# Scans two blocks ahead, a new order of ScalarE's copies, and three early expert jobs in one attention and mixture-of-experts kernel

## The chip, the cores and the metric

The kernel runs on one core of a Trainium2 chip. The metric is device time in microseconds (us), the median of the timed runs. Engines are named as the profile names them: PE is TensorE (PEld its weight loads), DVE VectorE, ACT ScalarE, POOL GpSimd, and SP the engine that issues most transfers.

## The reference

For 4 batches, 8 heads, 768 tokens and head dimension 48, a gated linear attention with a decay for each element, and then a mixture of 8 experts over the 384 columns of its output:

```python
for t in range(S):
    state = alpha[:, :, t, :, None] * state + np.einsum('bhd,bhe->bhde', k[:, :, t], v[:, :, t])
    y[:, :, t] = np.einsum('bhd,bhde->bhe', q[:, :, t], state)
...
fresh_e = int(np.argmax(logits[b, s]))
if s == 0 or local_gate[b, s] < 0.5:
    e = fresh_e
else:
    e = prev_e if prev_e >= 0 else fresh_e
...
h = np.maximum(x[b, s] @ w1[e], 0.0)
out[b, s] = p[e] * (h @ w2[e])
```

Each of the 3072 tokens goes to one expert (384 to 1024 to 384 columns), picked by its own logits or carried over from the token before, and is scaled with its softmax weight.

## The kernel before, in words

**Attention.** The tokens are cut into 24 blocks of 128 (two chunks of 64); block i belongs to batch i % 4, so a batch's state comes back every fourth block. The main loop makes 26 iterations, `for i in range(NB + 2)`, and keeps every instruction in the order in which it is written. One iteration touches several blocks:

- `scan1(i+1)`: POOL writes ones into four columns of the decay tile `a`; DVE scans the decays into `A` and takes reciprocals; POOL multiplies q by `A`.
- `kt(i)`, `pm(i)`: PE transposes k (kp), ACT copies it (kk); PE makes the products of k and q inside a chunk (pe), DVE masks them (pq).
- `scan2(i+1)`: DVE scans backwards into `sf`, POOL multiplies k by it.
- `xt(i-2)`: PE transposes the finished rows (xp), ACT copies them (xx); every fourth time a router `route(g)` starts.
- `ym(i-1)`: PE forms y from the states `sb` and from `pq`, ACT copies it to `XR`; SP stores it to `xd` in device memory.
- `um(i)`: PE forms the state update (up), DVE adds it to the state `st`, ACT copies the state to `sb` (two copies), and DVE starts the batch's next state.
- `first_v(i+1)`: ACT copies half of a v tile.

`load_a`, `load_x`, `load_v` are issued on SP for coming blocks; SP takes its queue in order.

**The router and the early jobs.** Three times in an iteration `other()` first emits what was put off in `later` (the low parts of splits, the stores of results), then one piece of each open router, then one piece of the early expert work; until there is such work, two matmuls on zeros (`dz`) stand in its place. A router works in 14 pieces over four blocks; its last ones scatter four blocks of list entries to `ls` (four indirect DMAs on POOL). When blocks 0 to 11 are listed, `early()` begins: it runs expert 0 and then expert 1 on the first C1 = 240 rows of their lists. A `Job` loads its list (SP), gathers token rows from `xd` (POOL), transposes them (tp) and splits them into xh and xl, and then runs `gemm1` (8 pieces of 9 matmuls) and `gemm2` (2 slices of 24 matmuls for 240 rows).

**Weights.** Each expert's weights come in 7 pieces (3 of w1, 128 x 1024, and 4 of w2, 128 x 768). Four raw buffers (`rw`) are shared; ACT casts a piece to the high part, and the low part is a subtraction, on POOL for w1 and on DVE for w2. Expert 0's pieces begin in block W0 = 4, one in each block, three asked for ahead; expert 1's begin in the second half of the first early job. There are four buffers for w1 parts and six for w2 parts.

**Expert phase.** After the loop come the remaining jobs with their own pools, in the order of the list in line 645: the rest of expert 1 (240 rows), experts 2 to 7 (480 rows each), the rest of expert 0. Here the order is not pinned.

Almost all operations pass through one wrapper, so the profile gives them line 78 (79 after the change); they are known by tile names.

## Time and profile before

| | us |
|---|---|
| timed runs | 541.92, 546.92, 548.57 (median 546.92) |
| the profiled execution's own time | 534.36 |
| its span, first to last instruction | 532.6 |
| first matmul of block 0 (kp), of block 20 | 13.34, 179.15 |
| last matmul | 519.28 |

Busy time over the span: PE 450.3 (85%), DVE 261.5 (49%), ACT 180.0 (34%), POOL 225.4 (42%); the mean granted clock of PE is 0.901.

How to read it: a busy share is an average over stages with different limits, so the span is cut into stages, and in each the engine that the others wait for is looked for. "Idle before, releaser" is the time that an engine stood before an instruction, and what ended it. The granted clock is the share of full speed that PE was given; at a low clock the same matmuls take longer and count as busy longer. Matmuls overlap, so the length of one is not its cost.

### The profile page before, as it was taken

The page shows a single profiled execution, that of the slowest core. Times are in us where ns is not written, and L with a number is a line of the kernel's source. Part 1 is how long each engine was busy: PE and PEld are TensorE (multiplying, and loading weights), DVE is VectorE, ACT ScalarE, POOL GpSimd, SP SyncE. Part 2 cuts the span into 40 slices and gives each one's busy share as a digit, 9 for nine tenths or more (in the row PEclk, how much of TensorE's full clock was granted, in tenths as well). Part 3 has the DMA queues.
Part 4 walks back from the last instruction along what each step waited for, and adds up shares of the span by engine and source line. Part 5 has one row for each costly group of instructions (what it writes and reads, how often), then busy time and mean ns, then how long its engine had stood idle before and what let it go on. Part 6 is the DMA issues. An engine that isn't in the chain of part 4 may idle for free. (4 is left out here: it accounts for less than half of the span.)

```text
span 532.6 us, 10859 instructions
## 1 busy us (share of the span) xinstructions
PE 450.3 (85%) x4391; PEld 404.1 (76%) x4391; DVE 261.5 (49%) x445; ACT 180.0 (34%) x350; POOL 225.4 (42%) x240
## 2 busy tenths in 40 slices
PE   4986879798686787963959989999999999999990
PEld 4764758576575676753949979999899998999990
DVE  3675696686887645263313443533425334243320
ACT  1243353434343333443103443342323433343110
POOL 6335344435254641093242637344372543633301
PEclk9898796789796688995878999999999999999996
DMA  9656465535455441376121545525345263360100
GB/s 204 131 162 233 138 200 137 142 108 142 130 164 124 135 87 43 122 185 173 50 53 53 163 138 148 179 74 167 117 122 174 84 189 115 103 191 14 46 3 25
DMA packets 30059, 66.15 MB, mean 124 GB/s; under 512 B 7694, under 2 KB 13979, under 8 KB 30007
## 3 DMA queue, kind: packets, MB, share of 16 engines
q1 hardware_dynamic: 23478, 54.42, 36.7%
q0 software_dynamic: 4864, 10.66, 6.9%
q8 instruction: 35, 0.57, 0.5%
q10 hardware_dynamic: 1665, 0.35, 0.4%
q14 instruction: 17, 0.14, 0.1%
HBM read 55.89 MB, written 10.70 MB: 125 GB/s over the span
## 5 line engine op out<-in xcount | busy, mean ns | idle before, releaser
L78 DVE SCALAR_TENSOR_TENSOR hl<-h,hh 128x480 fp32r<-128x480 f32 (+1 forms) x80 | 44.2, 554 | 80.4 <-ACT hh L78 80.4
L78 ACT ACTIVATE hh<-h 128x480 fp32r<-128x480 f32 (+1 forms) x80 | 39.0, 489 | 87.2 <-PE h L78 86.9
L78 POOL DMA_INDIRECT xg<-xd,li x32 | 35.2, 1099 | 50.4 <-DMA li<-ls 33.3
L78 POOL TENSOR_TENSOR x<-x,A 112x512 f32<-112x512 f32 x24 | 28.3, 1179 | 65.4 <-PE pe L78 16.7
L78 POOL DMA_INDIRECT out<-yo,li x32 | 33.5, 1048 | 50.1 <-DVE yo L78 44.2
L78 POOL TENSOR_TENSOR x<-x,sf 112x512 f32<-112x512 f32 x24 | 30.8, 1282 | 29.7 <-DVE sf L78 25.0
L78 DVE TENSOR_SCALAR yo<-yp,li 120x384 f32<-120x384 f32 x32 | 19.5, 616 | 47.0 <-PE yp L78 47.0
L78 ACT COPY sb<-st 48x384 f32<-48x384 f32 x48 | 24.5, 511 | 48.7 <-DVE st L78 48.1
L78 DVE TENSOR_TENSOR_SCAN A<-a,z 112x520 f32<-112x520 f32 x24 | 29.7, 1239 | 20.4 <-POOL a L78 18.9
L78 DVE TENSOR_TENSOR_SCAN sf<-a,z 112x520 f32<-112x520 f32 x24 | 37.8, 1574 | 0.0
L78 PE MATMUL h<-dz 128*128 128x240 f32 x138 | 34.7, 362 | 2.3 <-DVE z L78 2.3
L78 POOL DMA_INDIRECT ls<-pl,ix x24 | 24.0, 1000 | 26.0 <-DVE ix L78 19.3
L78 PE MATMUL xp<-cs,XR 128*128 128x128 f32 x72 | 15.8, 339 | 19.9 <-ACT kk L78 19.9
L78 PE MATMUL y<-vt,pq 64*64 64x48 f32 x768 | 32.4, 243 | 0.0
L78 DVE TENSOR_TENSOR st<-up,st 112x384 f32<-112x384 f32 (+1 forms) x24 | 12.5, 522 | 40.2 <-PE up L78 33.1
L78 PEld LDWEIGHTS y<-vt,pq 64*64 64x64 f32 x768 | 29.3, 158 | 3.6 <-issue 1.5
L78 PEld LDWEIGHTS h<-dz 128*128 128x128 f32 x138 | 24.3, 235 | 6.1 <-DVE z L78 2.3
L78 PEld LDWEIGHTS xp<-cs,XR 128*128 128x128 f32 x72 | 9.7, 166 | 22.9 <-ACT kk L78 22.7
L78 PE MATMUL y<-sb,x 112*64 112x96 f32 x384 | 26.1, 290 | 0.2 <-ACT sb L78 0.2
L78 PE MATMUL tp<-cs,xg 120*128 120x120 f32 x96 | 15.2, 290 | 13.0 <-DMA xg<-xd,li 7.1
L78 ACT COPY XR<-y 128x384 f32<-128x384 f32 x24 | 11.5, 479 | 42.1 <-PE y L78 42.1
L78 PEld LDWEIGHTS y<-sb,x 112*64 112x64 f32 x384 | 20.9, 164 | 5.7 <-issue 5.2
(229 smaller groups left out, 1260.0 us busy)
## 6 DMA issues: line engine op xcount, KB each, us to landing
x<-akq SPq DMA_DIRECT2D x24, 448.0 KB, 5.1
a<-akq SPq DMA_DIRECT2D x24, 227.9 KB, 4.5
vt<-vn SPq DMA_DIRECT2D x24, 192.0 KB, 2.4
xd<-XR SPq DMA_DIRECT2D x24, 192.0 KB, 4.2
rw_0a<-w SPq DMA_DIRECT2D x3, 512.0 KB, 5.8
rw_0a<-w SPq DMA_DIRECT2D x4, 384.0 KB, 4.9
rw_1a<-w SPq DMA_DIRECT2D x3, 512.0 KB, 4.2
rw_1a<-w SPq DMA_DIRECT2D x4, 384.0 KB, 5.9
```

The costliest lines, as they stand in the source:

```text
L78: r = f(*a, **k)
```

## The change

What it does:

1. **Scans.** The memset of `a` becomes a function of its own, `one_a`. In iteration i, `scan2(i+1)` comes first, then `one_a(i+2)`, and `scan1(i+2)` stands after the first `other()`: the decay scan runs two blocks ahead. `a` and `A` get three buffers, x five; `load_a` and `load_x` both fetch block i+3.
2. **Copies.** `um` ends with the add. The two copies of the state (`copies`) and the next state's start (`state`) are done for block i-1 in the next iteration, behind `kt(i)`. `first_v` moves ahead of `um`.
3. **y.** `ym` does the 16 products with `pq` first, and then the 8 with `sb`; the store to `xd` is issued by ACT right behind the copy to `XR`.
4. **Weights.** Expert 0's first four pieces are loaded in block 2, and used one per block from block 5. `Weights` has an argument for the engine of w1's low part: DVE for experts 0, 1 and 2, whose weights are begun inside the loop or by the early jobs. Expert 1's first four pieces are loaded when the early lists are.
5. **Early jobs.** There are three, in written order: expert 0, expert 1 (240 rows each), and the rest of expert 1, whose list is loaded when all routers are done. The transposes of the next job stand inside `gemm2` of the one before, through a PSUM tag of another block ("tr"). Expert 2's weights follow the first job, and the expert phase begins with expert 2. `other()` also gives only one piece at a time while a router is still open after the loop.

The diff, cut to its core:

```diff
-W0 = 4
+W0 = 2
 NP = 3
-NX = 4
+NX = 5
...
+    a_ = s_
...
-                self.defer(lambda e=g_ if n < 3 else v_, lo=lo, rw=rw, hi=hi:
+                self.defer(lambda e=self.sub if n < 3 else v_, lo=lo, rw=rw, hi=hi:
...
-            g_.memset(a[:, C + 1:SW:2 * (C + 1)], 1.0)
-            A = ap.tile([R, SW], F32, tag="A", bufs=2, name=f"A_{i}")
+            A = ap.tile([R, SW], F32, tag="A", bufs=3, name=f"A_{i}")
...
+        def one_a(i):
+            a = blk[i]["a"]
+            g_.memset(a[:, C + 1:SW:2 * (C + 1)], 1.0)
...
+        def copies(i):
+            sf, sb = blk[i]["s3"].rearrange("p c h d -> p c (h d)"), blk[i]["sb"]
             s_.copy(sb[64:112, :, 0, :], sf[64:112, 0:2])
             s_.copy(sb[0:48, :, 1, :], sf[0:48, 0:2])
...
             s_.copy(d["XR"], yw[:, 0:DM])
+            a_.dma_start(xd[1 + i * 128:1 + (i + 1) * 128], d["XR"])
...
+        def begin(e):
+            EW[e] = Weights(e, f"{e}a", 4, later.append, v_)
+            for _ in range(4):
+                EW[e].load()
...
+            jobs = [Job(e, r, n, m1, pp, 2, 2, 8, 2, (0, 1, 1), rows, 1, later.append)
+                    for e, r, n, rows in ((EARLY[0], 0, C1, 1 + T1 * 128), (EARLY[1], 0, C1, 1 + T1 * 128),
+                                          (EARLY[1], C1, CAP - C1, NTOK + 1))]
...
+                    if k % 4 < 2 or k == 2:
+                        next(ws, None)
+                    if nx and k > 3:
+                        if nx.r0 and k == 4:
+                            while steps:
+                                yield False
+                            nx.load_list()
+                        if nx.r0 and k == 5:
+                            nx.gather()
+                        if k == (7 if nx.r0 else 5):
+                            for _ in nx.trans():
+                                yield True
...
+                if n == 0:
+                    begin(NEXT)
...
         for i in range(NB + 2):
             if i + 1 < NB:
-                scan1(i + 1)
+                scan2(i + 1)
+            if i + 2 < NB:
+                one_a(i + 2)
             if i < NB:
                 kt(i)
+            if 0 < i <= NB:
+                copies(i - 1)
+                state(i - 1)
+            if i < NB:
                 pm(i)
-            if i + 1 < NB:
-                scan2(i + 1)
-            if i + 2 < NB:
-                load_a(i + 2)
             if i > NB:
                 drained[0] = True
             other()
+            if i + 2 < NB:
+                scan1(i + 2)
+            if i + 3 < NB:
+                load_a(i + 3)
+                load_x(i + 3)
...
+            if i == W0:
+                begin(EARLY[0])
+                wsteps = EW[EARLY[0]].steps()
+            elif i > W0 + 2:
+                next(wsteps, None)
             other()
             if i < NB:
                 um(i)
-            if 0 < i <= NB:
-                y_.dma_start(xd[1 + (i - 1) * 128:1 + i * 128], blk[i - 1]["XR"])
```

Where it moves instructions, in the names that follow the number behind a tile's name is the block, the router's group or the weight piece; x is the tile of k and q.

POOL, where the second router's four scatters (`ls`) fall, before:

```order
L78 TENSOR_TENSOR x_14_1416<-x_14_1416,A_14_1552 112x512
L78 TENSOR_TENSOR x_14_1416<-x_14_1416,sf_14_1582 112x512
L78 DMA ls_77<-pl_1_1480,ix_1_1587 24960x3 x4
L78 MEMSET a_15_1585 112x4
L78 TENSOR_TENSOR x_15_1522<-x_15_1522,A_15_1682 112x512
```

and now:

```order
L79 TENSOR_TENSOR x_14_1386<-x_14_1386,A_14_1490 112x512
L79 TENSOR_TENSOR x_14_1386<-x_14_1386,sf_14_1554 112x512
L79 MEMSET a_15_1494 112x4
L79 DMA ls_77<-pl_1_1481,ix_1_1588 24960x3 x4
L79 TENSOR_TENSOR x_15_1496<-x_15_1496,A_15_1596 112x512
L79 TENSOR_TENSOR x_15_1496<-x_15_1496,sf_15_1684 112x512
```

The memset of block 15's decays stood behind the scatters and now stands ahead of them; behind them now stands the q product of block 15, while PE is at block 13.

DVE, one turn of the loop near the same place, before (pq of block 12):

```order
L78 TENSOR_TENSOR st_11_963<-up_11_1421,st_11_963 112x384
L78 SCALAR_TENSOR_TENSOR st_15_1433<-st_11_963,A_11_1227 112x192
L78 SCALAR_TENSOR_TENSOR A_13_1443<-a_13_1375,z1_84 112x520
L78 RECIPROCAL z2_85<-A_13_1443 112x4
L78 TENSOR_TENSOR pq_12_1471<-pe_12_1454,cs_66 128x512
L78 SCALAR_TENSOR_TENSOR sf_13_1473<-a_13_1375,z2_85 112x520
```

and now (pq of block 13):

```order
L79 TENSOR_TENSOR st_12_1105<-up_12_1539,st_12_1105 112x384
L79 SCALAR_TENSOR_TENSOR sf_14_1554<-a_14_1384,z2_85 112x520
L79 SCALAR_TENSOR_TENSOR st_16_1567<-st_12_1105,A_12_1274 112x192
L79 TENSOR_TENSOR pq_13_1586<-pe_13_1569,cs_66 128x512
L79 TENSOR_TENSOR ps_1_1589<-pw_1_1549,ps_0_1127 128x40
L79 TENSOR_TENSOR po_1_1591<-ps_1_1589,oh1_105 128x32
L79 TENSOR_REDUCE ix_1_1588<-po_1_1591 128x4
L79 SCALAR_TENSOR_TENSOR A_15_1596<-a_15_1494,z1_84 112x520
L79 RECIPROCAL z2_85<-A_15_1596 112x4
```

The scan A is now of the block two ahead of pq and stands after the router's steps; the scan sf stands right behind the add, with the next state's start (st_16) between it and pq.

ACT, where the first weight piece is cast (w1h_0a_0), before:

```order
L78 COPY sb0_97<-st_4_247 48x2x192 x2
L78 COPY vt2_95<-vt2_95 64x384
L78 CAST w1h_0a_0_632<-rw1_0a_0_626 128x1024
L78 COPY kk_5_645<-kp_5_640 128x448
L78 COPY xx_0_380<-xp_3_674 128x384
L78 COPY XR_4_704<-y_4_679 128x384
```

and now:

```order
L79 COPY kk_5_646<-kp_5_641 128x448
L79 COPY sb0_97<-st_4_268 48x2x192 x2
L79 COPY xx_0_389<-xp_3_681 128x384
L79 COPY XR_4_711<-y_4_686 128x384
L79 DMA xd_76<-XR_4_711 128x384
L79 COPY vt0_91<-vt0_91 64x384
L79 CAST w1h_0a_0_716<-rw1_0a_0_425 128x1024
L79 COPY lc_0_733<-lg_0_720 128x128
```

The cast stood ahead of kk of block 5 and now stands behind block 5's kk, behind the store that ACT issues itself; the copies of sb follow kk.

## The prediction

> **What bounds the kernel now.** I read the table of stages first, cut at the matmuls that open blocks 0, 5, 13 and 20 (kp), at the end of the last block's work, and at the steady expert phase. Each row gives the stage and its length in us, then busy us (and instructions) of PE, PE's weight loads, DVE, ACT and POOL, then PE's granted clock, DMA share and GB/s.

> ```profile
> 13.34:44.28 30.94, 26.91 (x491) 21.96 (x492) 21.90 (x29) 11.33 (x24) 12.82 (x19) 0.93 0.55 142
> 44.28:119.16 74.88, 59.44 (x939) 49.42 (x938) 54.98 (x89) 29.94 (x65) 33.42 (x35) 0.79 0.55 162
> 119.16:179.15 59.99, 44.77 (x811) 36.96 (x809) 44.18 (x76) 22.58 (x55) 29.84 (x35) 0.85 0.54 140
> 179.15:229.40 50.25, 43.30 (x612) 37.23 (x612) 24.69 (x58) 19.98 (x44) 14.94 (x18) 0.87 0.36 101
> 229.40:293.00 63.60, 44.39 (x278) 41.41 (x279) 22.88 (x54) 15.46 (x36) 26.18 (x23) 0.79 0.38 96
> 320.00:520.00 200.00, 199.62 (x1108) 188.00 (x1105) 75.70 (x120) 66.77 (x108) 84.06 (x59) 1.00 0.39 115
> ```

> From 320 us on PE is full and at full clock; nothing there changes but names. The losses lie before 293: PE is idle and its clock is low. In the same view, block by block, the blocks without routing or weights (the first two rows) take 6.35 and 6.56 us; the third row is the block in which the first weights begin, the fourth one with a routing scatter.

> ```profile
> 31.37:37.72 6.35, 5.50 (x112) 4.53 (x110) 4.76 (x6) 2.82 (x6) 2.53 (x4) 1.00 0.59 170
> 37.72:44.28 6.56, 5.50 (x111) 4.52 (x110) 4.76 (x7) 2.82 (x6) 2.48 (x5) 1.00 0.59 172
> 44.28:57.61 13.33, 8.45 (x137) 6.94 (x135) 4.60 (x7) 4.13 (x8) 4.79 (x4) 0.74 0.68 219
> 126.12:137.56 11.44, 6.06 (x114) 5.01 (x113) 7.11 (x15) 3.19 (x8) 6.15 (x8) 0.85 0.62 164
> ```

> So a smooth block is 0.85 us above its PE work, and a disturbed one loses 5 to 7 us. The timeline of the scatter's block says why (start, length, engine, operation, and in brackets the idle time before it and its releaser):

> ```profile
> 125.81 1.05 POOL L78 DMA_INDIRECT ls<-pl,ix  x1 [1.08 <-DVE ix L78]
> 129.71 0.97 POOL L78 DMA_INDIRECT ls<-pl,ix  x1 [0.30 <-issue]
> 130.67 0.13 POOL L78 MEMSET a<- 112x4 f32 x1
> 130.84 1.24 DVE L78 TENSOR_TENSOR_SCAN A<-a,z 112x520 f32<-112x520 f32 x1 [4.06 <-POOL a L78]
> 134.57 1.17 POOL L78 TENSOR_TENSOR x<-x,sf 112x512 f32<-112x512 f32 x1 [1.18 <-DVE mx L78]
> 134.60 1.18 DVE L78 TENSOR_TENSOR ge<-L,mx 128x32 f32<-128x32 f32 x1
> 135.82 0.19 DVE L78 TENSOR_TENSOR ge<-ge,cs 128x32 f32<-128x32 f32 x1
> 136.74 0.60 PE L78 MATMUL rp<-cs,kr 128*32 128x128 f32 x2 [4.59 <-DVE kr L78]
> ```

> Four scatters hold POOL from 125.81 to 130.67; a four-column memset stands behind them, the scan behind the memset, the router behind the scan, and PE loses 4.59 us. The two `ge` rows show a second thing: the same operation takes 0.19 us alone, but 1.18 us when POOL's multiply (134.57 to 135.74) is running.

> **The change part by part.** *Scans two ahead.* The memset now precedes the scatters, and the scan and decay product of block i+2 are made in iteration i. What then waits for a scatter is POOL's q product, a block before PE needs it: 130.67 - 125.81 = 4.9 us of scatter against some 6.5 us of slack. I cost the scatter at nothing; if the cover is gone it costs the old 4 us, four times. What is late next is DVE's own turn, below.

> The floor of a block is PE's work at full clock plus the smooth 0.85. Blocks 13 to 19: 44.77 x 0.85 = 38.1, over 7 blocks 5.4, so 6.3 each. I add 0.7 for routing, whose DVE steps (134.60 to 136.69, half of it lock) still stand between pq and the next scan: 7.0 x 7 = 49, against 59.99. **Gain 11.** Bounds: 16 with nothing added, 2 if DVE sets the pace.

> DVE's turn of a block comes from these groups (mean ns of one) and POOL's two products:

> ```profile
> L78 DVE TENSOR_TENSOR_SCAN sf<-a,z 112x520 f32<-112x520 f32 x24 | 37.8, 1574 | 0.0
> L78 DVE TENSOR_TENSOR_SCAN A<-a,z 112x520 f32<-112x520 f32 x24 | 29.7, 1239 | 20.4 <-POOL a L78 18.9
> L78 POOL TENSOR_TENSOR x<-x,A 112x512 f32<-112x512 f32 x24 | 28.3, 1179 | 65.4 <-PE pe L78 16.7 <-issue 14.5 <-PE kp L78 12.6
> L78 DVE TENSOR_TENSOR pq<-pe,cs 128x512 f32<-128x512 f32 x24 | 16.1, 672 | 7.6 <-PE pe L78 7.5
> ```

> `sf` alone is as long as `A`; its mean of 1574 is a wait for the q product. In the new order: sf 1.24, state 0.36 to 0.47, pq 0.67, A 1.24, then the product 1.18, with the add of st inside it: 4.8 us if state gets in ahead of POOL's k product, 6.0 if it waits that out. With about 0.9 of routing that is 5.7 to 6.9, near PE's 6.3: DVE is the engine to watch. I take the lower, because state stands directly behind sf on DVE, while POOL first has to be signalled.

> [...]

> *First weights from block 2.* Before, the first weight is asked for and used in one block:

> ```profile
> 44.18 1.86 SPq L78 DMA_DIRECT2D rw_0a<-w  x3
> 49.23 1.04 ACT L78 CAST w1h_0a<-rw_0a 128x1024 fp32r<-128x1024 f32 x1 [3.06 <-DMA rw_0a<-w]
> 28.74 1.14 PE L78 MATMUL y<-vt,pq 64*64 64x48 f32 x32
> 50.76 0.90 PE L78 MATMUL xp<-cs,XR 128*128 128x128 f32 x3 [4.88 <-ACT kk L78]
> 53.07 1.95 PE L78 MATMUL y<-vt,pq 64*64 64x48 f32 x32
> 62.22 3.46 DVE L78 TENSOR_TENSOR ge<-L,mx 128x32 f32<-128x32 f32 x1
> 63.30 2.34 POOL L78 TENSOR_TENSOR w1l_0a<-rw_0a,w1h_0a 128x1024 fp32r<-128x1024 f32 x1
> ```

> ACT waits 3.06 us for the transfer with kk behind it, PE loses 4.88 us and goes on at a low clock (1.95 us for a y group that took 1.14 at 28.74). Asked for three blocks earlier, that wait goes. The three subtractions of 2.34 us leave POOL (one holds DVE's `ge` for 3.46 us) and become DVE's: a 768-wide one takes 0.93 us there (row below), so 1.24 each for 1024, and all seven steps now stand behind scan A and thus behind the q product.

> ```profile
> L78 DVE TENSOR_TENSOR w2l_0a<-rw_0a,w2h_0a x4: 925/928/932, 79.4 to 108.4; 128x768 fp32r<-128x768 f32 x4
> ```

> Blocks 5 to 12: 59.44 x 0.79 = 47.0, 5.9 a block, 6.7 with 0.85; plus about 1.2 for the subtraction and its lock: 7.9 x 8 = 63, against 74.88. **Gain 12**; bounds 21 with nothing added, 0 if lock and clock stay. The four loads (1.9 MB) now go ahead of block 6's inputs in SP's queue; block 5 lost 7 us to such a collision and ACT's wait together, so up to 4 of it may return. It is inside the bounds.

> *ACT's order, y's order, stores on ACT.* kk now precedes the two copies of sb, and y begins with the 16 products that don't need sb; both hide under PE's 0.85 and cost nothing. The store leaves SP for ACT:

> ```profile
> L78 SPq DMA_DIRECT2D xd<-XR x24: 319/379/3215, 23.4 to 226.7; - x24
> DMA to landing us min/median/max: 1.9/4.2/6.1
> ```

> Issue 0.38 us on ACT, which is busy 2.82 of 6.35: hidden, with 3 us to spare. In exchange the second expert's loads no longer stand in SP's queue behind stores. Start: one more scan (1.24 us) ahead of the first add: **1 us lost**.

> *Blocks 20 to 23 and the last xt, ym.* 43.30 x 0.87 = 37.7, plus 2 us for 12 more matmuls of the first job, plus 6 x 0.85: 45 against 50.25. **Gain 5**, bounds 0 and 8.

> *The tail.* Where the first early job ends, PE waits three times:

> ```profile
> 241.54 0.86 PE L78 MATMUL tp<-cs,xg 120*128 120x120 f32 x3 [5.91 <-DVE xl L78]
> 249.21 0.83 ACT L78 CAST w2h_2b<-rw_2b 128x768 fp32r<-128x768 f32 x1 [6.04 <-DMA rw_2b<-w]
> 251.40 0.57 PE L78 MATMUL h<-xh,w1h_1a 128*128 128x240 f32 x1 [5.44 <-DVE hl L78]
> 260.97 1.02 POOL L78 DMA_INDIRECT ls<-pl,ix  x1 [15.85 <-DVE ix L78]
> 276.51 1.43 PE L78 MATMUL tp<-cs,xg 120*128 120x120 f32 x6 [5.03 <-DMA xg<-xd,li]
> ```

> and the granted clock of the second wait and behind the third, by stages:

> ```profile
> 246.00:251.40 5.40, 0.00 (x1) 0.00 (x1) 1.33 (x3) 1.91 (x4) 0.00 (x0) 0.50 0.51 203
> 276.50:284.20 7.70, 6.66 (x29) 6.04 (x30) 1.95 (x4) 1.75 (x4) 5.33 (x5) 0.50 0.45 128
> ```

> The first two are ACT standing at weights that have not landed, and PE then runs at 0.50. Expert 1's weights are now begun some five blocks earlier, and expert 2's casts stand in the third job, not ahead of the second job's Relu: 5.91 + 5.44 and about 4 of slow clock go, of which I leave 2 standing. The third wait is a chain of four scatters, list, gather (260.97 to 276.51, 15.5 us) behind the last routing; the third job needs the same list, so its 5 us stay. New: at the first job of the expert phase ACT has two w2 casts that need the third job's last matmul, then four xh casts and a w1 cast: about 5 us, where the present kernel loses little. 5.91 + 5.44 + 4 - 2 = 13.4, less these 5, plus the 2 us of matmuls done earlier: **gain 10**; bounds 0 and 17. The third job itself is the same PE work as the first job of the expert phase was, so it moves no time of its own.

> Sum: 11 + 12 - 1 + 5 + 10 = **37 us** off the profiled execution, whose own time is 534.36 (span 532.6). The three timed runs have a median of 546.92, 2.4% above it; taking the same microseconds off gives **510**.

> **The rivals.** *A slow clock stays and DVE paces* (B): PE's busy time stays 59.44 and 44.77, and state and the subtractions wait out every product, 1.1 us more in 15 blocks. 59.44 + 8 x 0.85 and 44.77 + 7 x 0.85 save 18, of which 16 are lost again: 2 - 1 + 5 + 10 = 16 in all, **531**. For it: DVE has 54.98 of 74.88 now. Against: its waits are mostly those removed.

> *Full clock everywhere* (C): the bounds 16 and 21 hold, 16 + 21 - 1 + 5 + 10 = 51 in all, **496**. It needs PE gaps short enough to keep 1.00, as the two smooth rows with 0.85 us of gaps have. [...]

> *The waits only move* (E): B's blocks, and the tail's 10 come back at the list and at expert 2's weights: 16 - 10 = 6 off, **541**. It is also the case in which the lookahead is one in name only, because the a tiles land too late:

> ```profile
> a<-akq SPq DMA_DIRECT2D x24, 227.9 KB, 4.5
> ```

> Against that, a third buffer lets SP ask for a tile over a block (6 us) before its memset, and landing takes 4.5.

> *Slower* (D): ACT is in order, and at each store stands until an earlier transfer has landed. At 6.1 us, the longest landing, a block of ACT is 2.82 + 0.38 + 6.1 = 9.3 us, 1.8 over the forecast's mean of (49 + 63) / 15 = 7.5, and 24 blocks take 43 us more: **553**. ACT sets the pace from a hold of 4.3 us, the present time is passed at 5.8, and 2% over it at 6.3. Against it: the awaited transfers are some two blocks old.

> **How the numbers follow.** Forecast 0.58, B 0.16, C 0.12, E 0.07, D 0.07. About 2% can be told from no change, here 11 us: below 536 is faster. Faster: 0.58, 0.12 of B, 0.12: 0.82. Same: 0.04 of B, 0.07, 0.03 of D: 0.14. Slower: the rest of D, 0.04. The range, 491 to 533, takes in C and most of B and leaves E and D out.

> **What would show it.** Right: no idle of DVE behind POOL's memset; scatter blocks within 1.5 us of smooth ones; no ACT wait on rw_0a or rw_2a with PE idle; kp of block 20 some 22 us earlier; a 5 us wait of PE for the third job's gather still there. Wrong: block time set by DVE's subtractions behind POOL, a clock under 0.85 before block 20, or ACT idle at its stores.

## The result and the profile after

The changed kernel takes 511.94 us, median of four runs (508.97 to 513.86), against 544.42 for four runs of the kernel before (538.47 to 548.57): ratio 0.947, 95% interval 0.937 to 0.958, faster. The profiled executions lie closer together: 513.54 after (span 511.7) and 534.36 before. The times below are of single executions unless a ratio stands with them. Executions of one program differ by up to 3%, the longer ones at a lower granted clock (those of the kernel before that ran beside e12 go from 532.94 us at 0.904 to 548.62 at 0.874); ratios leave the slow ones out, and the profiled executions of e1 and e11 are slow ones.

The table of stages of the changed kernel, cut at the same events as before (kp of blocks 0, 5, 13 and 20, the last router matmuls lg, then a piece of the tail and the steady phase):

```profile
12.72:42.05 29.33, 27.06 (x491) 22.60 (x492) 21.06 (x29) 12.12 (x25) 12.97 (x19) 0.89 0.84 234
42.05:98.02 55.97, 51.52 (x939) 43.05 (x938) 48.23 (x89) 30.61 (x65) 26.21 (x32) 0.91 0.68 185
98.02:148.04 50.02, 44.79 (x811) 36.95 (x809) 37.12 (x77) 21.56 (x49) 28.00 (x33) 0.90 0.60 167
148.04:207.98 59.94, 43.99 (x623) 36.74 (x623) 27.34 (x63) 22.65 (x50) 17.64 (x21) 0.91 0.37 95
207.98:271.60 63.62, 49.78 (x291) 46.47 (x291) 22.55 (x54) 15.39 (x34) 22.35 (x23) 0.81 0.31 86
299.00:500.00 201.00, 199.68 (x1105) 188.05 (x1103) 74.57 (x117) 65.43 (x105) 84.81 (x60) 1.00 0.38 114
```

Blocks 0 to 4 went from 30.94 to 29.33 us, blocks 5 to 12 from 74.88 to 55.97, blocks 13 to 19 from 59.99 to 50.02. Kp of block 20 stands 31.1 us earlier (148.04 for 179.15). Then the stage from block 20 to the last lg, 229.39 - 179.15 = 50.2 us before, takes 59.9: 9.7 of it are lost again. From there to the end it is 303.7 us for 303.2: the tail gained nothing.

In the attention blocks the forecast waits are gone. The scatter's block, from the timeline (start, length, engine, operation, idle before it and releaser):

```profile
103.30 1.23 DVE L79 TENSOR_TENSOR_SCAN A<-a,z 112x520 f32<-112x520 f32 x1
104.17 1.22 POOL L79 DMA_INDIRECT ls<-pl,ix  x1 [1.04 <-DVE ix L79]
108.31 0.97 POOL L79 DMA_INDIRECT ls<-pl,ix  x1 [0.30 <-issue]
112.59 1.23 DVE L79 TENSOR_TENSOR_SCAN A<-a,z 112x520 f32<-112x520 f32 x1
```

Neither scan has idle time of DVE ahead of it (4.06 us before). In the view of waits (total in us, times, longest) for 42 to 148 us, DVE's for the memset are down to the first row. ACT, from 12 us on, stands behind its stores for up to 0.4 us at a time, as the second row says, and once for 2.0 us (third row, at 37.15), for which PE does not wait:

```profile
DVE A L79 <- POOL a L79: 1.0, 2, 0.5
ACT vt L79 <- ACT XR L79: 6.4, 16, 0.4
ACT vt L79 <- DMA xd<-XR: 2.0, 1, 2.0
```

A smooth block now takes what PE's matmuls take, with nothing above it:

```profile
120.19:125.93 5.74, 5.74 (x116) 4.96 (x115) 5.57 (x14) 2.92 (x6) 2.75 (x5) 1.00 0.73 195
```

What is left in these blocks is of another kind. The timeline at block 7, and two stretches, one up to the fall of the clock and one behind it:

```profile
54.92 1.18 POOL L79 TENSOR_TENSOR x<-x,A 112x512 f32<-112x512 f32 x1 [2.28 <-PE kp L79]
55.05 2.12 DVE L79 TENSOR_TENSOR w1l_0a<-rw_0a,w1h_0a 128x1024 fp32r<-128x1024 f32 x1
57.10 0.55 DVE L79 TENSOR_TENSOR st<-up,st 112x384 f32<-112x384 f32 x1
57.68 1.03 ACT L79 COPY sb<-st 48x384 f32<-48x384 f32 x2 [2.08 <-DVE st L79]
58.77 0.88 PE L79 MATMUL y<-sb,x 112*64 112x96 f32 x16 [1.50 <-ACT sb L79]
```

```profile
54.26:60.40 6.14, 4.64 (x101) 3.90 (x101) 6.02 (x10) 3.21 (x7) 2.44 (x3) 0.99 0.99 293
60.65:70.27 9.62, 9.62 (x114) 8.08 (x112) 7.43 (x13) 4.67 (x11) 3.86 (x6) 0.50 0.51 143
```

PE waits 1.50 us for sb, goes on at full clock, and 1.5 us later its clock falls to 0.50 and stays there for 9.6 us in which PE has no idle time at all. The wait costs 1.5 us; the half clock behind it costs 9.6 / 2 = 4.8. The rows above it say where the wait comes from: DVE's low-part subtraction runs beside POOL's q product and takes 2.12 us (the one at 197.61 takes 1.23), and the add of `st`, ACT's copy and PE stand behind it in turn.

To read this in all runs I cut the attention blocks (kp 0 to kp 20) into stretches of 0.5 us and added up the idle time of PE and, for each stretch, twice what the granted clock lacks of 1, which gives the time spent at half clock. Before: 34.7 us idle and 53.4 at half clock. After: 11.9 and 27.1. Half clock costs only where PE works: 6.7 of the 53.4 us were idle time as well, and 0.5 of the 27.1. So the gain has two parts: 23 us of waits, and 20 us of work at half clock, worth 10. (They add up to 33 for a stage that became 30.5 shorter; the modelled ends of the matmuls blur both.)

Where the time was given back, at block 20, from the timeline of SP, POOL, DVE and PE:

```profile
142.16 1.84 SPq L79 DMA_DIRECT2D rw_1a<-w  x4
144.25 1.13 POOL L79 DMA_INDIRECT xg<-xd,li  x1 [2.13 <-DMA li<-ls]
153.52 0.83 PE L79 MATMUL tp<-cs,xg 120*128 120x120 f32 x3 [4.25 <-DMA xg<-xd,li]
155.93 1.24 DVE L79 TENSOR_TENSOR_SCAN A<-a,z 112x520 f32<-112x520 f32 x1 [2.33 <-POOL a L79]
157.30 0.50 DVE L79 TENSOR_TENSOR xl<-tp,xh 128x360 fp32r<-128x360 f32 x1
157.86 0.90 PE L79 MATMUL xp<-cs,XR 128*128 128x128 f32 x3 [3.51 <-DVE xl L79]
158.69 1.95 PE L79 MATMUL y<-vt,pq 64*64 64x48 f32 x32
```

The first early job's transposes (tp) stand in PE's order ahead of rows that have not landed, 9.3 us after POOL asked for the first of them. Its tile tp is in the PSUM tag tr, one buffer, which kp and xp also use (before it was yp). So xp waits until DVE has made xl out of tp, and xl stands on DVE behind a scan that waits for POOL. Block 20 takes 17.6 us, block 21 13.1.

The tail has the waits that were forecast for the third job's gather and for the first job of the expert phase, and small ones, of which the first row is one, where the two large ones of 5.91 and 5.44 us were:

```profile
213.22 0.53 PE L79 MATMUL tp<-cs,xg 120*128 120x120 f32 x3 [1.85 <-DVE xl L79]
245.03 0.86 PE L79 MATMUL tp<-cs,xg 120*128 120x120 f32 x3 [3.26 <-DMA xg<-xd,li]
247.07 0.86 PE L79 MATMUL tp<-cs,xg 120*128 120x120 f32 x3 [1.17 <-DVE xl L79]
272.62 0.81 PE L79 MATMUL tp<-cs,xg 120*128 120x120 f32 x6 [0.76 <-issue]
274.88 0.53 PE L79 MATMUL tp<-cs,xg 120*128 120x120 f32 x3 [1.46 <-DVE xl L79]
277.62 1.46 PE L79 MATMUL tp<-cs,xg 120*128 120x120 f32 x6 [2.21 <-DVE xl L79]
```

By the same sums, over the 91 us from the last lg on, PE's idle time went from 20.8 to 18.3 us and its time at half clock from 27.3 to 30.7.

### The profile page after: what moved, and what is told of

It reads as the page before. It is cut to its first block, busy times and chain, and to the rows that moved or that the text cites. A ratio compares the mean times of both kernels' runs of the same rounds, so it can differ in the third digit from the quotient of the medians.

```text
span 511.7 us, 10818 instructions
## 1 busy us (share of the span) xinstructions
PE 445.2 (87%) x4391; PEld 398.6 (78%) x4391; DVE 248.3 (49%) x454; ACT 182.1 (36%) x350; POOL 205.5 (40%) x231
## 4 chain that ended last, share of the span: by engine, by line
PE 62%; issue 12%; DVE 10%; DMA 5%; ACT 4%; POOL 3%; another core or an unknown queue 1%; ACTq 0%; POOLq 0%; DVEq 0%; SPq 0%
PE h L79 25%; PE yp L79 20%; PE y L79 7%; PE up L79 2%; DVE A L79 2%; PE tp L79 2%; PE pe L79 2%; DMA vt<-vn 1%; DMA xd<-XR 1%; POOL x L79 1%; PE xp L79 1%; DMA tk<-tok 1%; DMA rw_3b<-w 1%; DVE st L79 1%
## 5 line engine op out<-in xcount | busy, mean ns | idle before, releaser
L79 POOL DMA_INDIRECT out<-yo,li x32 | 33.3, 1042 | 89.9 <-DVE yo L79 60.6
L79 POOL TENSOR_TENSOR x<-x,sf 112x512 f32<-112x512 f32 x24 | 29.0, 1208 | 38.7 <-DVE sf L79 38.7
L79 POOL TENSOR_TENSOR x<-x,A 112x512 f32<-112x512 f32 x24 | 30.1, 1255 | 30.6 <-PE kp L79 7.5
L79 DVE TENSOR_TENSOR_SCAN A<-a,z 112x520 f32<-112x520 f32 x24 | 29.7, 1236 | 15.8 <-POOL a L79 15.7
L79 PE MATMUL h<-dz 128*128 128x240 f32 x138 | 33.2, 347 | 2.7 <-DVE z L79 2.3
L79 DVE TENSOR_TENSOR_SCAN sf<-a,z 112x520 f32<-112x520 f32 x24 | 35.4, 1476 | 0.1
L79 PEld LDWEIGHTS y<-vt,pq 64*64 64x64 f32 x768 | 27.3, 145 | 7.0 <-issue 6.8
L79 ACT COPY sb<-st 48x384 f32<-48x384 f32 x48 | 24.5, 510 | 12.7 <-DVE st L79 12.1
L79 PEld LDWEIGHTS h<-dz 128*128 128x128 f32 x138 | 22.9, 221 | 7.2 <-DVE z L79 2.3
L79 PE MATMUL tp<-cs,xg 120*128 120x120 f32 x96 | 15.5, 296 | 15.0 <-DMA xg<-xd,li 7.5
L79 PE MATMUL y<-sb,x 112*64 112x96 f32 x384 | 23.1, 268 | 4.8 <-ACT sb L79 4.8
L79 DVE TENSOR_TENSOR st<-up,st 112x384 f32<-112x384 f32 (+1 forms) x24 | 12.4, 517 | 29.9 <-PE up L79 20.1
L79 PEld LDWEIGHTS tp<-cs,xg 120*128 120x128 f32 x96 | 11.9, 154 | 18.0 <-DVE xl L79 7.7
L79 PE MATMUL up<-vt,kk 128*48 128x96 f32 (+1 forms) x384 | 24.6, 274 | 0.5 <-issue 0.5
L79 PEld LDWEIGHTS y<-sb,x 112*64 112x64 f32 x384 | 18.3, 147 | 6.7 <-ACT sb L79 5.6
## 6 DMA issues: line engine op xcount, KB each, us to landing
a<-akq SPq DMA_DIRECT2D x24, 227.9 KB, 5.2
rw_0a<-w SPq DMA_DIRECT2D x3, 512.0 KB
rw_1a<-w SPq DMA_DIRECT2D x3, 512.0 KB
```

Of the source, the lines that this page charges most:

```text
L79: r = f(*a, **k)
```

## The experiments

Each is the changed kernel with the edit shown, run beside the kernel before on the same chip; ratios are to that kernel, with 95% intervals. The changed kernel itself stands at 0.947 (0.937 to 0.958). In the table, a is kp 0 to kp 20, s is kp 20 to the last lg, t is the rest of the span, idle is PE's idle time in a, and half its time at half clock there, all in us of the profiled execution.

| run | edit | median | ratio | a | s | t | idle | half |
|---|---|---|---|---|---|---|---|---|
| before | | 544.4 | 1 | 165.8 | 50.2 | 303.2 | 34.7 | 53.4 |
| after | | 511.9 | 0.947 | 135.3 | 59.9 | 303.7 | 11.9 | 27.1 |
| e1 | scans one block ahead | 533.4 | 0.984 | 158.6 | 62.8 | 302.7 | 20.5 | 66.6 |
| e2 | first weights from block 4 | 512.0 | 0.951 | 135.6 | 59.7 | 299.4 | 14.7 | 23.4 |
| e3 | w1 low parts on POOL | 511.0 | 0.947 | 138.5 | 56.9 | 301.8 | 14.8 | 33.3 |
| e4 | expert 1's loads later | 511.8 | 0.952 | 134.1 | 58.5 | 301.0 | 14.8 | 20.5 |
| e5 | tp in yp | 504.3 | 0.941 | 133.3 | 55.7 | 296.3 | 15.5 | 24.3 |
| e6 | e4 and e5 | 499.5 | 0.929 | 137.3 | 52.7 | 296.6 | 21.8 | 20.4 |
| e7 | two routing steps a piece | 510.6 | 0.950 | 134.9 | 56.8 | 304.0 | 21.4 | 12.1 |
| e8 | all orders and weights undone | 531.9 | 0.988 | 162.2 | 59.4 | 300.1 | 27.5 | 60.1 |
| e9 | copies of sb undone | 533.1 | 0.981 | 153.5 | 59.4 | 304.2 | 19.6 | 52.7 |
| e10 | y, store, first_v undone | 525.3 | 0.967 | 148.6 | 60.8 | 305.0 | 16.0 | 49.5 |
| e11 | e6, gather a block later | 512.6 | 0.940 | 134.8 | 54.5 | 314.3 | 11.8 | 28.1 |
| e12 | e6, two early jobs | 503.0 | 0.933 | 136.2 | 58.9 | 297.4 | 17.7 | 17.0 |

Taking from a the idle time and half of the working time at half clock leaves 107 to 110 us in all fourteen traces. So in the attention blocks the runs differ in these two things and in next to nothing else.

**e1, the scans.**

```diff
-        one_a(1)
-        scan1(1)
...
-                scan2(i + 1)
-            if i + 2 < NB:
-                one_a(i + 2)
+                one_a(i + 1)
+                scan1(i + 1)
             if i < NB:
                 kt(i)
...
                 pm(i)
+            if i + 1 < NB:
+                scan2(i + 1)
...
-            if i + 2 < NB:
-                scan1(i + 2)
```

> The changed kernel with the scan, its memset and its decay product made one block ahead again; all else as changed. Theory: the lookahead takes the scatters out of DVE's way, so undoing it brings back a DVE wait of about 4 us behind the memset in each block with scatters and some 2 us of PE idle and slow clock in others: 16 us lost, about 528 against 512. Rival (the weights and ACT's order made the attention stage faster, the lookahead little): within 4 us of the changed kernel, 512 to 516, and no DVE wait over 3 us behind POOL's memset.

Ratio 0.984 (0.978 to 0.989), 3.7% of the kernel before, or 20 us, above the changed kernel: the theory. DVE's wait behind the memset is back, twice (4.30 and 4.53 us), and PE's for the router behind it; here the first of DVE's two, the line of PE's waits from 42 to 171 us, the longest stretch at half clock, and PE's rows where it begins:

```profile
84.95 1.24 DVE L79 TENSOR_TENSOR_SCAN A<-a,z 112x520 f32<-112x520 f32 x1 [4.30 <-POOL a L79]
```

```profile
PE rp L79 <- DVE kr L79: 7.9, 4, 2.4
```

```profile
85.30:119.30 34.00, 32.56 (x375) 27.62 (x378) 24.39 (x44) 12.05 (x25) 11.60 (x14) 0.50 0.41 106
```

```profile
84.75 0.34 PE L79 MATMUL y<-vt,pq 64*64 64x48 f32 x5 [0.38 <-issue]
85.48 0.65 PE L79 MATMUL y<-vt,pq 64*64 64x48 f32 x9 [0.38 <-issue]
```

Blocks 13 to 19 take 59.0 us, as before the change (60.0). The size came by another road than the expectation's 4 us a block: PE's idle time grows by 8.6 us only, its time at half clock by 39.5, of which 34 in one piece. Ahead of that piece PE had stood only in three short gaps beside the scatters, of 0.23 us and the two shown, which the profile puts down to nothing it sees. So this trace does not show that the scans' place brought the 34 us on; that undoing it costs time is shown by the ratio, which does not rest on this one execution. The third buffers and the earlier loads of a and x stay in every run, so their share is not known.

**e2, the first weights.**

```diff
-W0 = 2
+W0 = 4
...
-            elif i > W0 + 2:
-                next(wsteps, None)
+            next(wsteps, None)
```

> The changed kernel with the first expert's weights asked for and first cast in iteration 4, as before; all else as changed (low parts still on DVE). Theory: ACT's wait of 3 us for rw_0a with PE idle for about 5 us returns once, with a few us of slow clock behind it: 6 to 9 us lost, about 519. Rival (the wait only moved into collisions of the early loads with the x tiles; undoing costs nothing): 510 to 514, blocks 3 to 5 shorter by what block 6 loses.

Ratio 0.951 (0.940 to 0.961): the rival's number. The wait itself came back as the theory had it:

```profile
44.29 1.04 ACT L79 CAST w1h_0a<-rw_0a 128x1024 fp32r<-128x1024 f32 x1 [3.09 <-DMA rw_0a<-w]
45.82 0.90 PE L79 MATMUL xp<-cs,XR 128*128 128x128 f32 x3 [2.98 <-ACT kk L79]
```

Block 5 takes 12.1 us in place of 6.8, the stage of blocks 5 to 12 59.3 for 56.0, and blocks 13 to 19 only 47.0 for 50.0. One wait of 3 us with 6.8 us of half clock costs what some other stretch of half clock in the changed kernel costs; in the sum it can't be told from nothing.

**e3, the subtractions.**

```diff
-            EW[e] = Weights(e, f"{e}a", 4, later.append, v_)
+            EW[e] = Weights(e, f"{e}a", 4, later.append, g_)
```

> The changed kernel with the low parts of w1 of the three early experts subtracted on POOL again (2.3 us each on POOL for about 1.2 on DVE); all else as changed. Theory of the prediction (DVE is the engine to watch, the subtraction on DVE costs about 1.2 us a block with its wait): no loss for the three blocks, 508 to 513. Rival (POOL is the engine that holds the scans): each of the three products on POOL delays x and its scan by 2 us, and the w1 parts of experts 1 and 2 stand ahead of scatters and gathers: 4 to 8 us lost, about 518.

Ratio 0.947 (0.940 to 0.955): no loss in the total. DVE's scan does take longer beside POOL: sf takes 4.15 us for 1.23 and ends 1.09 us after POOL's subtraction does (57.75 to 60.10), and PE stands for the router's em behind it. At 64.38 sf takes 4.15 us again, beside POOL's q product (63.94 to 65.12) and the next subtraction (65.08 to 67.44).

```profile
57.04 4.15 DVE L79 TENSOR_TENSOR_SCAN sf<-a,z 112x520 f32<-112x520 f32 x1
57.75 2.35 POOL L79 TENSOR_TENSOR w1l_0a<-rw_0a,w1h_0a 128x1024 fp32r<-128x1024 f32 x1
62.43 0.24 PE L79 MATMUL rb<-cs,em 32*128 32x32 f32 x1 [1.65 <-DVE em L79]
```

17.1 us of half clock follow, from 63.1 us on. So in either place one subtraction costs PE a wait (1.50 us in the changed kernel) and half clock behind it: blocks 5 to 12 take 60.4 us for 56.0, blocks 13 to 19 48.8 for 50.0, and in the total the two places can't be told apart.

**e8, e9, e10, the orders.** e8 undoes the places of the copies of sb and the state, y's order, the store on SP, first_v and the weights' start; e9 only the first of these, e10 the y, the store and first_v.

```diff
-                copies(i - 1)
-                state(i - 1)
...
                 um(i)
+                copies(i)
+                state(i)
```

```diff
-            a_.dma_start(xd[1 + i * 128:1 + (i + 1) * 128], d["XR"])
...
                 um(i)
+            if 0 < i <= NB:
+                y_.dma_start(xd[1 + (i - 1) * 128:1 + i * 128], blk[i - 1]["XR"])
+            if i + 1 < NB:
+                first_v(i + 1)
```

The first is e9; the second, with the products of q and sb ahead of those of pq and v again, is e10; e8 is both and e2's.

> The changed kernel with ACT's copies of sb behind the update, the order of y, the store of the rows on SP, first_v and the first weights (iteration 4) as they were before; the scans two ahead, the low parts of w1 on DVE and the early jobs as changed. Theory (the scans are most of the gain in the attention blocks; the orders cost and bring nothing): at most 3 us above the run with the weights alone put back, 511 to 515. Rival (the orders let PE go on while ACT and DVE are behind and are worth as much as the scans): 520 or more, with PE idle behind sb in each block.

> The changed kernel with ACT's two copies of sb and DVE's state behind each block's update again, ahead of the next block's kk; y's order, the stores on ACT, the weights from block 2, the scans and the early jobs as changed. Theory (formed on e8: with the scans ahead, DVE's st stands behind two scans and a product, so an ACT that must first copy sb cannot give PE its kk): PE waits for kk in most blocks, some 2 us each, and the total comes to within 4 us of e8, 528 to 536. Rival (the store, first_v or y's order made the 20 us of e8): 511 to 516.

> The complement: y's order, the store on SP and first_v's place as before, the two copies and the state where the change has them. Theory (the copies' place is the whole of e8's loss): 510 to 515, PE's waits for sb at y a few us larger at most. Rival (y's order with the copies late is what lets PE go on, or SP's queue is held by the stores): 518 or more, PE idle ahead of y by about 1 us a block.

Ratios 0.988 (0.978 to 0.998), 0.981 (0.974 to 0.989) and 0.967 (0.961 to 0.973). The theory that the orders cost and bring nothing fell with e8. e9 answers to the theory formed on it in the total (its waits for kk are 1.2 us each, not 2), and e10 to its rival (0.5 us a wait, not 1): both the copies and the rest matter, 3.6% and 2.0% of the changed kernel's time. With e8 at 4.3% the intervals are too wide to say whether the two add up. PE's waits from 42 us on (to 148 us in e8, to 160 in e9 and e10), first of the kernel before (44 to 179 us), then of e8, e9 and e10; the 4.9 and the 6.8 are the ones for the first weights, which e8 puts back too:

```profile
PE xp L78 <- ACT kk L78: 17.0, 12, 4.9
```

```profile
PE xp L79 <- ACT kk L79: 19.1, 11, 6.8
```

```profile
PE xp L79 <- ACT kk L79: 13.5, 11, 2.5
```

```profile
PE y L79 <- ACT sb L79: 7.2, 14, 1.7
```

In e9 kk stands on ACT behind sb, and sb behind a DVE that has scans in front of st. In e10 y begins with the products that need sb. The changed kernel has no wait for kk in its view for 42 to 148 us, and 2.9 us of waits for sb. In e9 and e10 PE's sums of idle are only 8 and 4 us over the changed kernel's; behind them stand some 50 us of half clock for 27. One wait of e10 and what follows it:

```profile
63.28 0.88 PE L79 MATMUL y<-sb,x 112*64 112x96 f32 x16 [1.69 <-ACT sb L79]
```

```profile
65.60:85.70 20.10, 20.10 (x239) 17.05 (x242) 12.60 (x26) 7.49 (x16) 7.51 (x11) 0.50 0.51 149
```

Of e10's three parts I did not try each alone.

**e4, e5, e6, block 20.** e4 moves one line; e5 gives the first job's transposes the tile they had before; e6 is both.

```diff
-            begin(EARLY[1])
...
             for _ in jobs[0].trans():
                 yield True
+            begin(EARLY[1])
```

```diff
-                tp = self.ps.tile([128, 3, SL], F32, tag="tp" if self.pb[0] else "tr", bufs=self.pb[0] or 1,
+                tp = self.ps.tile([128, 3, SL], F32, tag="tp" if self.pb[0] else self.tt, bufs=self.pb[0] or 1,
...
+            jobs[0].tt = "yp"
             for _ in jobs[0].trans():
```

> The changed kernel with the four loads of expert 1's weights (1.9 MB) asked for behind the first early job's transposes, not between its lists and its gather. Theory (the loads collide with the gather, which took 9 us from issue to use where others land in 3.3): PE's wait of 4.25 us for xg and the 3.51 us behind it shrink to under 2 in all, block 20 takes about 11 us in place of 17.6, the total is about 505. Rival (the list and the gather are late by their own chain, and the job is simply begun too soon): the 4 us wait stays, 510 to 514.

> The changed kernel with the transposes of the first early job written to the PSUM tile yp (free until that job's second multiplication, and used for it before the change), not to the tile tr that kp and xp of the attention blocks share; all else as changed. Theory (block 20 stalls because xp must wait until DVE has taken xl out of the shared tile): PE's wait of 3.5 us ahead of xp goes, and the slow y behind it (1.95 for 1.14 us), 5 us in all, about 507. Rival (the gather's late landing alone sets the block; DVE's xl is only the next thing in the same delay): the wait for xg stays at 4 us or grows, 511 to 514.

> The same, and expert 1's loads asked for behind the first job's transposes as in e4. Theory (two causes in a row, of which removing the first in e4 only let the second wait grow from 3.5 to 4.4): with both gone block 20 takes 9 to 11 us in place of 17.6, the stage from block 20 to the last router matmul about 51 in place of 60, the total about 504. Rival (a third thing holds the block, POOL's memset behind the two gathers, DVE's scan behind it): block 20 stays over 13 us, the total at 509 or more.

In e4 (0.952, 0.944 to 0.959) the gather's wait shrank and the next one grew in its place:

```profile
148.95 0.50 PE L79 MATMUL tp<-cs,xg 120*128 120x120 f32 x3 [1.34 <-DMA xg<-xd,li]
153.80 0.90 PE L79 MATMUL xp<-cs,XR 128*128 128x128 f32 x3 [4.35 <-DVE xl L79]
```

So the loads do delay the gather (4.9 us from POOL's second request to the transposes, where it was 7.8), and it does not pay alone. e5 (0.941, 0.932 to 0.950) has the theory's direction and 504.3 for the expected 507. e6 gives 499.5 (ratio 0.929, 0.921 to 0.938), 4.5 us under the theory's 504, the lowest of the study: it beats the kernel before and the changed one. Its stage from block 20 is 52.7 us, near the theory's 51, but block 20 still takes 13.0 us and block 19 11.8, since POOL now stands at the list's landing with the next memset behind it, the third thing that the rival named:

```profile
145.60 1.14 POOL L79 DMA_INDIRECT xg<-xd,li  x1 [5.38 <-DMA li<-ls]
149.40 1.01 PE L79 MATMUL kp<-cs,x 112*128 112x112 f32 x4 [5.10 <-POOL a L79]
153.79 0.86 PE L79 MATMUL tp<-cs,xg 120*128 120x120 f32 x3 [2.32 <-DMA xg<-xd,li]
```

**e11, the gather later.** This is e6 with two things more: the later start, and a memset that holds each early gather at its place on POOL.

```diff
             yield False
             yield False
+            yield False
+            yield False
+            yield False
             jobs[0].gather()
...
+                if pinned[0]:
+                    g_.memset(xg[:, 0:1], 0.0)
```

> e6 with the first job's two gathers and transposes one block later, and every early gather held at its written place on POOL (by a one-column memset of its tile ahead of it); the lists are asked for as before. Theory (in e6 POOL stood 5.4 us at the list's landing with x's product and the next memset behind it, and PE waited 5.1 us for them and 2.3 us for the gather): these waits go, block 19 takes 7 to 8 us in place of 11.8 and block 20 8 to 9 in place of 13; the early job ends later by what it starts later, so of the 7 us 4 to 6 stay: about 495 against 499.5. Rival (the list lands later still when the block goes faster, and the wait moves with it, or the later start is paid back whole at the end of the jobs): 498 to 502.

Slower than both theories: 512.6, ratio 0.940 (0.932 to 0.949). The waits did go (blocks 19 and 20 take 6.0 and 5.0 us), but blocks 21 and 22 take 14.9 and 15.6 us (10.5 and 9.7 in e6), and the tail is longer. Of the tail's 314 us only the direction can be taken, and the memset's share was not tried apart. As tried here, starting the job later did not pay for the waits that it removed.

**e7, the routing chain.**

```diff
-            for r in list(steps):
-                if next(r, 0) == 0:
+            for r in list(steps) * (2 if drained[0] else 1):
+                if r in steps and next(r, 0) == 0:
```

> The changed kernel with two routing steps in place of one between pieces of the early jobs, once the attention blocks are done; all else as changed. Theory (the third job's wait for its gather is the routing chain of the last four blocks, spread over as many pieces as it has steps): the last scatters start some 8 us earlier, the wait of 3.3 us for xg and part of the low clock behind it go, 4 us gained, about 508. Rival (the chain is bound by its own latencies, and PE then idles at the routing's matmuls instead): 511 to 515.

The last scatters began 14.1 us after the last lg where it was 23.3, and the wait for xg went; the total stayed (0.950, 0.940 to 0.960). In its place, DVE and PE:

```profile
228.13 0.17 DVE L79 TENSOR_TENSOR gt<-cntp,cs 8x22 f32<-8x22 f32 x1 [7.00 <-DMA ls<-pl,ix]
229.50 0.57 PE L79 MATMUL h<-xh,w1h_1a 128*128 128x240 f32 x1 [6.15 <-DVE hl L79]
```

An operation of the overflow count, which the scheduler put behind the routing, waited 7.00 us, by the profile for the scatters, in front of hl. Neither theory had it; whether the chain without that operation would gain the 4 us stays open.

**e12, two early jobs.** This is e6 with expert 1's second half at the head of the expert phase again; expert 2's weights are begun there too, which the lines below leave out.

```diff
-                                          (EARLY[1], C1, CAP - C1, NTOK + 1))]
...
-    for e in [e for e in range(E) if e not in EARLY] + list(EARLY[:-1]):
+    for e in [EARLY[-1]] + [e for e in range(E) if e not in EARLY] + list(EARLY[:-1]):
```

> e6 with two early jobs in place of three: expert 1's second half is the first job of the expert phase again, expert 2's weights are loaded and cast there, as before the change. It tells where the tail's forecast gain of 10 went. Theory A (the third job's early place moves no time: the wait for the list and the gather stands ahead of whichever job comes next, and expert 2's casts cost about the same in either place): within 4 us of e6, 496 to 504, the tail from the last router matmul 293 to 301. Theory B (what eats the gain is the new stop at the first job of the expert phase, some 4.5 us of PE idle and a low clock behind it, which exists only with three early jobs): faster than e6 by 5 to 9 us, 491 to 495. Theory C (the third job early does fill PE and hides expert 2's casts): slower than e6 by 5 us or more, 505 or above.

503.0, ratio 0.933 (0.926 to 0.940) against e6's 0.929 (0.921 to 0.938), the tails 297.4 and 296.6: theory A. The wait for the routing's list stands ahead of whichever job is next, and where the third job runs moves no time that can be told.

## Why the prediction was right and where it was wrong

The number was right, 510 for 511.94; the sum behind it was not, and that the two meet is in good part luck. Off the profiled execution the forecast was 37 us, measured are 534.36 - 513.54 = 20.8; the medians lie 32.5 apart, and the stages missed in opposite directions:

- *Scans, blocks 13 to 19: forecast 49, measured 50.0.* Right in size and cause: e1 puts back 59.0, and e8, where the scans are the main thing left in the attention blocks, has 51.4. DVE did not set the pace. One sign failed: scatter blocks are 2 to 5 us above smooth ones, not 1.5. One term did too: a smooth block has no 0.85 above PE's work.
- *First weights, blocks 5 to 12: forecast 63, measured 56.0.* The stage gained 19 us, not 12, and mostly not by the weights: with them put back (e2) it is 59.3 and the total the same. The waits for rw_0a went as forecast. What the step missed is that this stage too hung on the scans (69.3 in e1) and on ACT's order (70.5 in e9).
- *Low parts on DVE, 1.2 us a block with the lock: seen in one block, not in each.* No run shows a lock of the two engines as a rule, as the sums for routing and for this step have it; what the changed kernel's trace shows is single operations that take longer beside a product of POOL, and others that don't. The three subtractions of expert 0 begin while POOL's q product runs (1.18 us each, from 47.42, 54.92 and 61.54), end 1.1 us after it, and take 1.42, 2.12 and 1.73 us where one with POOL idle (197.61) takes 1.23; pq beside the k product at 58.87 takes 0.68 us, as it does elsewhere (0.67 in the prediction's row). The router's ge, 0.19 us alone, takes 0.35, 1.20, 0.75 and 0.37 us beside the k product (52.29, 83.37, 110.94, 138.30). The longest subtraction brings the 1.50 us wait of block 7, and 9.6 us of half clock follow; the sum had a price for the subtraction and none for what follows. On POOL (e3) the same thing happens, so neither place gains.
- *"ACT's order, y's order, stores on ACT: cost nothing".* This step failed most. They cost nothing, but much of the gain hangs on them: without them and the early weights (e8) 20 of the 32 us are lost. I priced what they add and not what they free, although the view of PE's waits before the change has it as its largest row (shown at e8): 17.0 us behind kk, of which only 4.88 are the first weights'. The rest is kk standing behind the copies of sb, and the 0.85 that the sum left on every smooth block holds such a wait (0.84 to 1.06 us in blocks 2 to 4). With the scans ahead and the copies in their old place (e9), 13.5 us of such waits are there again.
- *The start, 1 us lost: 2.2 gained* (kp 0 at 12.72 for 13.34, blocks 0 to 4 1.6 shorter, each in one execution).
- *Blocks 20 to 23, gain 5: 9.7 lost.* The step counted matmuls and smooth blocks, and left out that the job's transposes move into the tile tr, where xp and kp queue behind DVE's xl, and that POOL's gathers stand ahead of a memset. e5 and e6 show it: 59.9, 55.7, 52.7.
- *The tail, gain 10: none* (303.7 for 303.2). Right were the third job's wait (3.26 + 1.17 for 5) and the new stop at the expert phase (0.76 + 1.46 + 2.21 for 5). The 5.91 and 5.44 went, but five smaller waits between 208 and 230 us came in their place (1.76, 1.85, 1.57, 0.96 and 0.90, 7.0 in all), and the half clock, of which I let 2 of 4 us go, grew by 3.4 us. e5 and e6, with 17.1 us of half clock there in place of 30.7, have the tail 7 us shorter.

So 31 us in the attention blocks for 22, and 10 lost for 15 gained behind them. The rival of ACT held at its stores (D) is refuted: ACT stands 0.4 us at a time there, once 2.0, and D needed 4.3 in every block. B and C were both half right: the clock stays low in places and is full in others.

Behind much of the misses stands the clock, which I treated as an average over a stage. In these runs half clock comes in pieces of 3.4 us or multiples: 10.2, 3.4 and 6.8 us in the changed kernel's blocks 5 to 19 (the first behind the wait of block 7, the other two behind gaps beside scatters, for which see the last section); 20.5 in e10; 34 in e1. The prediction's rows have smooth blocks at 1.00 and a gap of 4.88 us with slow work behind it; half clock followed far shorter waits, one of 1.50 us that ended at 58.77 and one of 1.69 us that ended at 63.28 in e10. So each small wait is a chance of losing several microseconds. Blocks 5 to 19 of the kernel before spent 48.5 us at half clock.

## What to carry to other kernels

Price a wait on PE's path at its length plus the half clock that may follow: here waits of 1.50 and 1.69 us were followed by 9.6 and 20 us at half speed, and in e9 and e10 8 and 4 us more of idle time came with attention blocks 18 and 13 us longer. An order that "costs nothing" must be asked what it frees. Read the table of waits for the engine that paces the stage row by row, the many short ones too, before a part of a change is priced at nothing. When a loop is run further ahead, go through each engine's order for what now stands late in it, and move the consumers' copies with it. When work is moved into a loop, look at which single-buffered tile it shares with the loop, and which of its transfers the loop's own memsets and loads queue behind.

## What the runs showed of the hardware

Half clock held for 20.1 us in e10 and for 34.0 us in e1 although PE was busy for 20.10 and 32.56 of them; sustained work did not bring the full clock back within one or two pieces of 3.4 us. In the fourteen traces 177 pieces at half clock (kp 0 to 300 us) had PE busy throughout; 126 of them were followed by full clock, 51 by more half clock. What decides it is open.

In some executions PE stands for short times while POOL's scatters run. In the changed kernel's block 14, where "issue" says that nothing which the profile shows held it:

```profile
108.51 0.33 PE L79 MATMUL y<-vt,pq 64*64 64x48 f32 x4 [0.42 <-issue]
109.24 0.38 PE L79 MATMUL y<-vt,pq 64*64 64x48 f32 x6 [0.40 <-issue]
110.01 0.78 PE L79 MATMUL y<-vt,pq 64*64 64x48 f32 x18 [0.39 <-issue]
```

Gaps of 0.4 us come every 0.75 us, the first (at 107.00) 2.8 us after the first of the four scatters, and 3.4 us of half clock follow; four more beside the third router's scatters (133.56 to 135.76) come with 6.8 us of it, from 135.39 on. The profiled executions of e1, e2, e4, e10 and e12 have such rows in two or three scatter blocks; those of e5, e6 and e7, with the same attention blocks as the changed kernel, have none, and their block 14 takes 7.1 us for 9.3. The cause was not tried.
